# Weights from 64-bit floats: upper bits of the low word by ScalarE, and the first gates' low halves by TensorE

## The chip, the cores and the metric

One NeuronCore of a Trainium2 chip runs the whole program. The metric is device time in microseconds (us), from launch to end. The engines are named as the profile names them: PE (TensorE, matmuls; PEld are its weight loads), DVE (VectorE), ACT (ScalarE), POOL (GpSimd) and SP (SyncE, which issues the transfers).

## The reference, cut to what matters

```python
def _attn_ref(q, k, v, alpha):                 # B=4, H=8, S=768, D=48
    for t in range(S):
        state = alpha[:, :, t, :, None] * state + np.einsum('bhd,bhe->bhde', k[:, :, t], v[:, :, t])
        y[:, :, t] = np.einsum('bhd,bhde->bhe', q[:, :, t], state)

def _moe_ref(x, w_in, conv_w, w_out):          # d_model 384, d_ff 1024, 3 taps
    h = np.maximum(x @ w_in, 0.0)
    # conv_out: 3 taps of h along the sequence, one weight per feature and tap
    gate = 1.0 / (1.0 + np.exp(-conv_out))
    return h * gate @ w_out

def _moe2_ref(x, g_ln, w_ch1, w_ch2):          # hidden 1536
    xn = (x - mu) / np.sqrt(var + 1e-06) * g_ln
    return x + np.maximum(xn @ w_ch1, 0.0) @ w_ch2
```

The three functions follow one another. The four weight matrices and `conv_w` reach the kernel as 64-bit floats; the kernel makes 32-bit floats of them itself.

## The kernel before, in words

The 3072 rows of the sequence are 12 blocks of 256. Attention runs ahead of the blocks in 24 chunks of 128 rows: two scans and a reciprocal on DVE (L399, L405, L415), products on POOL (L411, L419), scores, outputs and state on PE (L441, L509, L525). Each block then goes through two halves. The first half has 8 pieces of 128 features (`moe1_a`, `moe1_gate`, `moe1_split`): nine products into a PSUM bank `h` (L595), relu in that bank (L608), one tap by ACT (L612) and two by DVE (L616), sigmoid (L635), `h` times gate in the bank (L639), a rounded upper half `gh` by ACT (L656), the rest `gl` by DVE (L661). Only then is the bank free, and there are three banks `h`. Six products per 128 features go into `acc` (L687). A norm and two transposes (L756) lead to the second half, with 12 pieces: nine products (L790), `gh` by ACT (L798), `gl` by DVE (L803), six products into `acc`.

All products use numbers split into a rounded upper half and a lower half. A weight matrix is cut in pieces of 768 columns: 4 of `w_in` (w1), 4 of `w_out` (w2), 6 each of `w_ch1` (w3) and `w_ch2` (w4), 20 in all. A piece is loaded as 64-bit numbers (L279) and converted (`from_f64`, `convert_weight`): ACT makes a scaled float of the high word (L254); DVE shifts it left by 3 (L257), joins the top 3 bits of the low word (L260) and the sign (L263); ACT rounds the upper half (L301). The lower half is a subtraction: for w1 and w2 by PE into PSUM with a copy by ACT (L305, L306, L309), for w3 and w4 by POOL (L312). Two buffers `z` hold pieces in work.

The order is written by a planner (`Plan`): every step has a price, a turn and its buffers, and steps are given to engines in the order of their turns as soon as their inputs and buffers are free by these prices. Each engine then runs its list strictly in that order. The turns come from the table of numbers at the top (`FIRST`, `LEAD`, `LOADS`, `CONVERT`, `WAIT` and so on).

Of the kernel before, what the change touches and what calls it, by code (L numbers as in the profile page):

```python
# [35 lines left out]
HB = 3  # L36
XB = 2
ZB = 2
GB = 3
RB, EB = 2, 2  # L40

SPLIT = 0
UNITS = (0, 0, 0), (0, 1, 0) 
XN = 1 
X1 = 2 
WAIT = 4
LAG = 5
FIRST = (-16,-15,-14,-4,2)
LEAD = 6
SPACING = 2  # L50
FETCH = 10
LOADS = -17, -12, -6, -5.5
LOAD_PACE = 1
CONVERT = (-13,-8,9,9)
CONVERT_PACE = 1, 1, 1
EARLY = 0
LATER = 0, 8
LOW2 = "pool"
LOWS = "pe", "pe", "pool", "pool"
# [144 lines left out]
def dve_us(n, rate=1):  # L204
    return 0.15 + 0.00104 * rate * n
# [11 lines left out]
def attn_moe_kernel(ctx: ExitStack, tc, qka, vv, qka_t, v_t, w_in, conv_w, w_out, g_ln, w_ch1, w_ch2, out):  # L217
# [32 lines left out]
    def from_f64(z, raw, n):  # L250

        low, high = raw[:, :n, 0], raw[:, :n, 1]
        zi = z.bitcast(I32)
        yield lambda: act.activation(out=z, in_=high.bitcast(F32), func=ACTF.Copy, scale=2.0 ** -112)  # L254

        def shift():
            dve.tensor_scalar(out=zi, in0=zi, scalar1=3, scalar2=None, op0=ALU.logical_shift_left)  # L257

        def more():
            dve.scalar_tensor_tensor(  # L260
                out=zi, in0=low, scalar=29, in1=zi, op0=ALU.logical_shift_right, op1=ALU.bitwise_or
            )
            dve.scalar_tensor_tensor(  # L263
                out=zi, in0=high, scalar=-(2 ** 31), in1=zi, op0=ALU.bitwise_and, op1=ALU.bitwise_or
            )

        yield shift
        yield more

    raw_w = {}  # L270

# [14 lines left out]
    def convert_weight(n, dst, j):  # L286
        m, w, z = PIECE * DM, (f"w{n}", j), ring("z", ZB)
        t = {}

        def first():  # L290
            t["z"] = wk.tile([128, m], F32, tag="z", name="z", bufs=ZB)
            raw = raw_w.pop((n, j)).rearrange("p j s f -> p (j s f)")
            t["f"] = list(from_f64(t["z"], raw.rearrange("p (n w) -> p n w", w=2), m))
            t["f"][0]()

        def high():
            t["w"] = weight_tile(n, j, F32R)
# [12 lines left out]

        def rest(engine):
            engine.tensor_tensor(out=t["w"][:, :, 1], in0=t["z"], in1=t["w"][:, :, 0], op=ALU.subtract)  # L312

        add("act", act_us(m), first, r=[w], new=[z])
        add("dve", dve_us(m, 0.5), lambda: t["f"][1](), w=[z], port=True)
        add("dve", 2 * dve_us(m), lambda: t["f"][2](), r=[w], w=[z], port=True)
        add("act", act_us(m), high, r=[z], w=[w])
        low = LOW2 if n > 2 and j >= F2 // 2 // PIECE else LOWS[n - 1]
        if low == "pe":
            for i in range(PIECE):  # L320
                b = ring("att", 2)
# [263 lines left out]
    def moe1_a(i, j):  # L585
        hb, cb = ring("h", HB), ring("cv", 2)
        t = h_t[i, j] = {"hb": hb, "cb": cb}

        def products():
            hi, lo = x_t[i]  # L590
            ps = bank("h", "h")
            n = 0
            for l, r in ((0, hi), (1, hi), (0, lo)):
                for k in range(K1):
                    pe.matmul(  # L595
                        out=ps[:, :T + 2], lhsT=w1[j][:, l, k * 128:(k + 1) * 128], rhs=r[:, k, :],
                        start=n == 0, stop=n == 3 * K1 - 1,
                    )
                    n += 1
            t["h"] = ps[:, :T + 2]  # L600

        def relu():
            if i < EARLY:
                ps = t["h"]
                t["h"] = wk.tile([128, T + 2], F32, tag="hs", name="hs", bufs=EB)
                act.activation(out=t["h"], in_=ps, func=ACTF.Relu)
            else:
                act.activation(out=t["h"], in_=t["h"], func=ACTF.Relu)  # L608
# [12 lines left out]
        xs = list(x_b[i]) if i in x_b else []
        add("pe", 9 * 0.000458 * (T + 2), products, r=xs + [("w1", j // PIECE)], new=[hb], mode="full")
        if i < EARLY:
            t["hb"] = ring("hs", EB)
            add("act", act_us(T), relu, r=[hb], new=[t["hb"]])
        else:
            add("act", act_us(T), relu, w=[hb])
        add("act", act_us(T, True), first_tap, r=[t["hb"]], new=[cb])
        add("dve", 2 * (dve_us(T) + 0.06), taps, r=[t["hb"]], w=[cb])

    def moe1_gate(i, j):
        t = h_t[i, j]

        def sigmoid():
            act.activation(out=t["cv"], in_=t["cv"], func=ACTF.Sigmoid)  # L635

        def times(engine):
            g = t["h"][:, 1:T + 1]
            engine.tensor_tensor(out=g, in0=g, in1=t["cv"], op=ALU.mult)  # L639

        add("act", act_us(T), sigmoid, w=[t["cb"]])
        if i < EARLY:
            add("pool", pool_us(T), lambda: times(pool), r=[t["cb"]], w=[t["hb"]], port=True)
        else:
            add("dve", dve_us(T), lambda: times(dve), r=[t["cb"]], w=[t["hb"]])
# [4 lines left out]
    def moe1_split(i, j):  # L650
        t = h_t.pop((i, j))
        m_b[0, i, j] = bh, bl = halves()

        def high():
            m_t[0, i, j] = [wk.tile([128, T], F32R, tag="gh", name="gh", bufs=GB), None]
            act.activation(out=m_t[0, i, j][0], in_=t["h"][:, 1:T + 1], func=ACTF.Copy)  # L656

        def rest(engine):
            hi = m_t[0, i, j][0]
            lo = m_t[0, i, j][1] = wk.tile([128, T], F32R, tag="gl", name="gl", bufs=GB)  # L660
            engine.tensor_tensor(out=lo, in0=t["h"][:, 1:T + 1], in1=hi, op=ALU.subtract)  # L661

        add("act", act_us(T), high, r=[t["hb"]], new=[bh])
        if i < EARLY:
            add("pool", pool_us(T), lambda: rest(pool), r=[t["hb"], bh], new=[bl], port=True)
        else:
            add("dve", dve_us(T), lambda: rest(dve), r=[t["hb"], bh], new=[bl])

    def parts_of(s, i):

# [76 lines left out]
    def ln3(i, t):  # L747
# [175 lines left out]
    def load_small():  # L923
# [234 lines left out]
```

## Time and profile before

| | us |
|---|---|
| median of 3 runs (689.48 to 691.96) | 691.35 |
| the profiled execution | 688.87 |
| its span, first to last instruction | 687.1 |
| PE busy | 643.6 (94%) |
| DVE busy | 449.5 (65%) |
| ACT busy | 308.8 (45%) |
| POOL busy | 127.1 (19%) |

Busy shares are means over the span. Whether an engine sets the pace is read per stretch: which engine is full there, and on whom PE waits. A matmul's duration includes its way through the pipeline, so what one costs in a stream is the distance between the starts of two.

### The profile page before, as it was taken

To read this page: it belongs to the slowest core of one execution; us is meant where nothing else is said; L and a number is where in the kernel's file an instruction comes from. 1 tells how busy PE (TensorE), PEld (TensorE's weight loads), DVE (VectorE), ACT (ScalarE), POOL (GpSimd) and SP (SyncE) were. 2 spreads that over 40 slices of the span, in tenths; PEclk is the share of its full clock that TensorE was granted. 3 is DMA by queue.
4 is the path that set the end of the run, shared out by engine and by line. 5 is a ranking of instruction groups with operands and counts; after the bars stand their busy time and mean duration, and the time that the engine had idled before them with its cause. 6 is when DMAs were issued, how large, how long until landed. Compare 5 with 4: busy or idle time off the path is not lost.

```text
span 687.1 us, 14178 instructions
## 1 busy us (share of the span) xinstructions
PE 643.6 (94%) x5754; PEld 609.2 (89%) x5754; DVE 449.5 (65%) x902; ACT 308.8 (45%) x752; POOL 127.1 (19%) x193
## 2 busy tenths in 40 slices
PE   3779868889999999999999999999999999999995
PEld 2557858789999999999999999999999999999994
DVE  5989998989749549639549548648648547365221
ACT  2758775445436336335335335345245245253210
POOL 4143244451320121201111111201201100000000
PEclk9999998979999999999999999999999999999998
DMA  9999101012310211110120111110100000000000
GB/s 303 307 359 298 55 0 42 16 41 79 98 56 24 58 57 39 57 42 24 56 56 25 57 57 44 57 37 30 55 14 24 18 1 24 1 24 1 2 24 27
DMA packets 15738, 44.51 MB, mean 65 GB/s; under 512 B 1473, under 2 KB 4673, under 8 KB 15665
## 3 DMA queue, kind: packets, MB, share of 16 engines
q1 hardware_dynamic: 15664, 43.52, 20.1%
q8 instruction: 47, 0.77, 0.5%
q14 instruction: 27, 0.21, 0.1%
HBM read 38.80 MB, written 4.72 MB: 63 GB/s over the span
## 4 chain that ended last, share of the span: by engine, by line
PE 83%; DVE 8%; ACT 3%; issue 2%; DMA 1%; POOL 1%; SPq 0%; ACTq 0%; DVEq 0%
PE acc L687 34%; PE h L790 22%; PE h L595 14%; PE y L509 5%; PE s L441 4%; DVE z L260 2%; DVE z L263 2%; PE u L525 2%; PE h L756 1%; DVE cv L616 1%; DMA raw<-in_qka 1%; PE kt L465 1%; DVE gl L661 1%; DVE z L257 1%; PE low L305 1%
## 5 line engine op out<-in xcount | busy, mean ns | idle before, releaser
L687 PE MATMUL acc<-w,gh 128*128 128x384 f32 x960 | 254.7, 346 | 3.0 <-ACT w L301 1.5
L687 PEld LDWEIGHTS acc<-w,gh 128*128 128x128 f32 x960 | 163.2, 190 | 7.3 <-ACT w L301 1.7
L687 PE MATMUL acc<-w,gl 128*128 128x384 f32 x480 | 162.5, 339 | 0.1
L803 DVE SCALAR_TENSOR_TENSOR gl<-h,gh 128x256 fp32r<-128x256 f32 x144 | 60.7, 423 | 153.7 <-ACT gh L798 153.0
L798 ACT ACTIVATE gh<-h 128x256 fp32r<-128x256 f32 x144 | 55.2, 384 | 195.9 <-PE acc L687 184.5
L790 PE MATMUL h<-xnh,w 128*128 128x256 f32 x864 | 129.2, 285 | 1.5 <-POOL w L312 1.5
L790 PEld LDWEIGHTS h<-xnh,w 128*128 128x128 f32 x864 | 119.4, 190 | 3.3 <-POOL w L312 1.8
L616 DVE SCALAR_TENSOR_TENSOR cv<-h,cw,cv 128x256 f32<-128x256 f32 x192 | 91.8, 481 | 28.8 <-ACT cv L612 24.4
L687 PEld LDWEIGHTS acc<-w,gl 128*128 128x128 f32 x480 | 91.1, 190 | 0.7 <-DVE gl L803 0.7
L595 PE MATMUL h<-xh,w 128*128 128x258 f32 x576 | 86.9, 286 | 4.7 <-DVE gl L661 2.9
L595 PEld LDWEIGHTS h<-xh,w 128*128 128x128 f32 x576 | 78.2, 189 | 8.8 <-DVE gl L661 4.8
L790 PE MATMUL h<-xnl,w 128*128 128x256 f32 x432 | 75.3, 283 | 0.0
L790 PEld LDWEIGHTS h<-xnl,w 128*128 128x128 f32 x432 | 62.2, 190 | 0.0
L635 ACT ACTIVATE cv<-cv 128x256 f32<-128x256 f32 x96 | 39.7, 415 | 37.1 <-DVE cv L616 36.8
L608 ACT ACTIVATE h<-h 128x258 f32<-128x258 f32 x96 | 35.5, 370 | 46.0 <-PE h L595 45.5
L402 POOL COPY ends<-later 112x4 f32<-112x4 f32 x24 | 4.9, 203 | 261.1 <-DVE later L399 259.5
L595 PE MATMUL h<-xl,w 128*128 128x258 f32 x288 | 50.1, 282 | 0.0
L612 ACT ACTIVATE cv<-h,cw 128x256 f32<-128x256 f32 x96 | 45.5, 474 | 1.9
L639 DVE TENSOR_TENSOR h<-h,cv 128x256 f32<-128x256 f32 x96 | 40.5, 424 | 5.9 <-ACT cv L635 4.0
L661 DVE TENSOR_TENSOR gl<-h,gh 128x256 fp32r<-128x256 f32 x96 | 40.1, 417 | 5.6 <-ACT gh L656 5.2
L656 ACT ACTIVATE gh<-h 128x256 fp32r<-128x256 f32 x96 | 36.7, 383 | 10.3 <-DVE h L639 9.1
L595 PEld LDWEIGHTS h<-xl,w 128*128 128x128 f32 x288 | 41.3, 190 | 0.0
(87 smaller groups left out, 742.6 us busy)
## 6 DMA issues: line engine op xcount, KB each, us to landing
raw<-in_qka SPq DMA_DIRECT2D x23, 673.8 KB, 4.8
w<-in_moe_w_ch SPq DMA_DIRECT2D x12, 768.0 KB, 16.5
vraw<-in_vv SPq DMA_DIRECT2D x24, 256.0 KB, 2.8
out<-x SPq DMA_DIRECT2D x11, 384.0 KB, 2.5
w<-in_moe_w_in SPq DMA_DIRECT2D x4, 768.0 KB, 11.4
w<-in_moe_w_out SPq DMA_DIRECT2D x4, 768.0 KB, 13.5
raw<-in_qka SPq DMA_DIRECT2D x1, 448.0 KB, 3.8
out<-x SPq DMA_DIRECT2D x2, 192.0 KB, 3.3
```

The source lines that it names most:

```text
L595: pe.matmul(out=ps[:, :T + 2], lhsT=w1[j][:, l, k * 128:(k + 1) * 128], rhs=r[:, k, :], start=n == 0, stop=n == 3 * K1 - 1,)
L608: act.activation(out=t["h"], in_=t["h"], func=ACTF.Relu)
L612: act.activation(out=t["cv"], in_=t["h"][:, 0:T], func=ACTF.Copy, scale=cw[:, 0, j:j + 1])
L616: dve.scalar_tensor_tensor(out=t["cv"], in0=t["h"][:, k:k + T], scalar=cw[:, k, j:j + 1], in1=t["cv"], op0=ALU.mult, op1=ALU.add,)
L635: act.activation(out=t["cv"], in_=t["cv"], func=ACTF.Sigmoid)
L639: engine.tensor_tensor(out=g, in0=g, in1=t["cv"], op=ALU.mult)
L656: act.activation(out=m_t[0, i, j][0], in_=t["h"][:, 1:T + 1], func=ACTF.Copy)
L661: engine.tensor_tensor(out=lo, in0=t["h"][:, 1:T + 1], in1=hi, op=ALU.subtract)
L687: pe.matmul(out=acc_t[s, i][t][:, :DM], lhsT=l[:, ts], rhs=w[j][:, r], start=j in firsts and n == 0, stop=j + 1 in lasts and n == 2,)
L790: pe.matmul(out=ps[:, :T], lhsT=w3[j][:, l, k * 128:(k + 1) * 128], rhs=r[:, k, :], start=n == 0, stop=n == 3 * K1 - 1,)
L798: act.activation(out=m_t[1, i, j][0], in_=u["ps"][:, :T], func=ACTF.Relu)
L803: dve.scalar_tensor_tensor(out=lo, in0=u["ps"][:, :T], scalar=0.0, in1=hi, op0=ALU.max, op1=ALU.subtract)
```

## The change

ACT takes over the top bits of the low word: it reads byte 3 of each 8-byte number, multiplies by 1/32 with an offset that makes the rounding a floor, and writes the integer over the low word. DVE's shift goes into the join, so two DVE instructions are left of three. In the first two blocks the lower half of `h` times gate is made by PE, which subtracts `gh` in the bank (`less`), and ACT copies the result to `gl`; the product with the gate is written from column 0 on. The lower halves of the first three pieces of w4 go from POOL to PE and ACT. There is a fourth buffer for `gh` and `gl`, and the table of turns has other numbers. The branch `EARLY`, off before, is gone.

```diff
-GB = 3
-RB, EB = 2, 2
+GB = 4
+RB = 2
-WAIT = 4
+WAIT = 6
-LEAD = 6
+LEAD = 4
...
-LOADS = -17, -12, -6, -5.5
+LOADS = -17, -16, -4, -9.5
-CONVERT = (-13,-8,9,9)
...
+CONVERT = -17, -9, 8, 10
+BY_PE = 2, 0
-LOWS = "pe", "pe", "pool", "pool"
+LOWS = "pe", "pe", "pool", "pe" 
...
-        def shift():
-            dve.tensor_scalar(out=zi, in0=zi, scalar1=3, scalar2=None, op0=ALU.logical_shift_left)
-
-        def more():
+        def top():
+            byte = raw[:, :n, :].bitcast(U8)[:, :, 3]
+            act.activation(out=low, in_=byte, func=ACTF.Copy, scale=1 / 32, bias=-15.5 / 32)
+
+        def join():
             dve.scalar_tensor_tensor(
-                out=zi, in0=low, scalar=29, in1=zi, op0=ALU.logical_shift_right, op1=ALU.bitwise_or
+                out=zi, in0=zi, scalar=3, in1=low, op0=ALU.logical_shift_left, op1=ALU.bitwise_or
             )
...
+    def less(ps, high):
+
+        pe.matmul(out=ps, lhsT=minus, rhs=high, start=False, stop=True, skip_group_check=True)
...
-            g = t["h"][:, 1:T + 1]
-            engine.tensor_tensor(out=g, in0=g, in1=t["cv"], op=ALU.mult)
+            dve.tensor_tensor(out=t["h"][:, :T], in0=t["h"][:, 1:T + 1], in1=t["cv"], op=ALU.mult)
...
+        if i < BY_PE[0] and not plan.direct:
+            add("pe", 0.000458 * T, take, r=[bh], w=[t["hb"]], mode="full")
+            add("act", act_us(T), lambda: rest(True), r=[t["hb"]], new=[bl])
         else:
```

ACT's list, where the third pieces of w1 and w2 are converted (`w1_2` and `w2_2` with a serial number; raw and converted tile have numbers of their own). Before:

```order
L254 ACTIVATE z_341<-w1_2_113 128x768
L309 ACTIVATE w2_1_331<-low_333 128x384
L309 ACTIVATE w2_1_331<-low_347 128x384
L254 ACTIVATE z_355<-w2_2_156 128x768
L388 ACTIVATE raw_183,low_68<-raw_183 112x4x128
L301 ACTIVATE w1_2_380<-z_341 128x2x384
```

The same pieces in the changed kernel (L257 is the scaled float, L261 the new instruction, L306 the upper half, L314 the copy of a lower half):

```order
L257 ACTIVATE z_326<-w1_2_122 128x768
L261 ACTIVATE w1_2_122<-w1_2_122 128x768
L306 ACTIVATE w2_1_333<-z_310 128x2x384
L314 ACTIVATE w2_1_333<-low_337 128x384
L306 ACTIVATE w1_2_350<-z_326 128x2x384
L314 ACTIVATE w2_1_333<-low_345 128x384
L257 ACTIVATE z_361<-w2_2_127 128x768
L314 ACTIVATE w1_2_350<-low_355 128x384
L261 ACTIVATE w2_2_127<-w2_2_127 128x768
```

Each piece now has one instruction more on ACT between the scaled float and the upper half, and DVE's join waits for it.

PE's list in the second block's first half, before: products into `h` (L595) alternate with products into `acc` (L687).

```order
L595 MATMUL h_923<-xh_443,w1_1_313 128x258 x6
L595 MATMUL h_923<-xl_452,w1_1_313 128x258 x3
L687 MATMUL acc_571<-w2_3_544,gh_906 128x384 x2
L687 MATMUL acc_571<-w2_3_544,gl_917 128x384
L687 MATMUL acc_572<-w2_3_544,gh_906 128x384 x2
L687 MATMUL acc_572<-w2_3_544,gl_917 128x384
L595 MATMUL h_956<-xh_443,w1_1_313 128x258 x6
L595 MATMUL h_956<-xl_452,w1_1_313 128x258 x3
```

The same place in the changed kernel (L354 is `less`, L604 the products into `h`, L310 and L311 the lower half of a piece of w4):

```order
L354 MATMUL h_883<-gh_963,minus_62 128x256
L604 MATMUL h_982<-xh_477,w1_1_302 128x258 x6
L604 MATMUL h_982<-xl_479,w1_1_302 128x258 x3
L310 MATMUL low_999<-z_930,ident_61 128x384
L311 MATMUL low_999<-w4_1_993,minus_62 128x384
L354 MATMUL h_906<-gh_997,minus_62 128x256
L604 MATMUL h_1016<-xh_477,w1_2_350 128x258 x6
L604 MATMUL h_1016<-xl_479,w1_2_350 128x258 x3
L354 MATMUL h_948<-gh_1026,minus_62 128x256
```

`h_982` takes the bank of `h_883`, and `h_1016` that of `h_906`: the nine products stand right behind the `less` on the bank that they reuse.

DVE's list at the last three pieces, before (L803 is `gl` of the second half):

```order
L257 TENSOR_SCALAR z_1423<-z_1423 128x768
L405 RECIPROCAL from_end_79<-later_1419 112x4
L260 SCALAR_TENSOR_TENSOR z_1423<-w4_4_520,z_1423 128x768
L263 SCALAR_TENSOR_TENSOR z_1423<-w4_4_520,z_1423 128x768
...
L257 TENSOR_SCALAR z_1484<-z_1484 128x768
L415 SCALAR_TENSOR_TENSOR a_1501<-raw_723,from_end_79 112x516
L260 SCALAR_TENSOR_TENSOR z_1484<-w4_5_566,z_1484 128x768
L263 SCALAR_TENSOR_TENSOR z_1484<-w4_5_566,z_1484 128x768
```

And in the changed kernel (L264 and L267 are the two joins, L736 belongs to the norm, L816 is `gl`):

```order
L264 SCALAR_TENSOR_TENSOR z_1390<-z_1390,w4_4_376 128x768
L267 SCALAR_TENSOR_TENSOR z_1390<-w4_4_376,z_1390 128x768
L736 SCALAR_TENSOR_TENSOR xn_1431<-x1_1305,mv_1374,gl_65 128x384
L816 SCALAR_TENSOR_TENSOR gl_1470<-h_1413,gh_1449 128x256
L264 SCALAR_TENSOR_TENSOR z_1411<-z_1411,w3_5_548 128x768
L267 SCALAR_TENSOR_TENSOR z_1411<-w3_5_548,z_1411 128x768
```

The shifts are gone, and the scans (L399, L415) that stood between the last pieces stand elsewhere.

## Rows read from the trace of the kernel before

**Rows 1.** Windows: busy time and count per engine, granted clock, DMA share, GB/s

```profile
core 0: us, PE busy (x) PEld busy (x) DVE busy (x) ACT busy (x) POOL busy (x), PEclk, DMA share, GB/s
0.00:46.20 46.20, 28.25 (x285) 19.52 (x285) 36.98 (x50) 22.28 (x39) 15.27 (x35) 0.93 0.99 327
46.20:97.70 51.50, 45.23 (x417) 39.58 (x418) 46.99 (x92) 38.58 (x88) 15.84 (x18) 1.00 0.48 148
97.70:149.10 51.40, 40.56 (x293) 37.47 (x291) 45.16 (x64) 24.08 (x47) 26.88 (x19) 0.83 0.07 20
149.10:687.10 538.00, 529.62 (x4764) 512.58 (x4762) 320.34 (x697) 223.84 (x580) 69.13 (x123) 1.00 0.13 39
```

**Rows 2.** PE's waits, first 150 us: line, releaser, total us, times, longest

```profile
PE h L756 <- DVE gl L661: 6.2, 1, 6.2
...
PE acc L687 <- ACT w L301: 1.5, 1, 1.5
...
PE h L790 <- POOL w L312: 1.5, 1, 1.5
...
PE acc L687 <- POOL w L312: 1.4, 1, 1.4
```

**Rows 3.** Windows of the two longest stretches at half the clock

```profile
102.80:109.60 6.80, 4.73 (x17) 4.64 (x18) 5.35 (x12) 3.48 (x9) 2.77 (x4) 0.50 0.01 4
136.90:147.20 10.30, 7.85 (x29) 7.56 (x30) 8.88 (x8) 2.92 (x4) 6.46 (x4) 0.50 0.00 0
```

**Rows 4.** Groups by line: count, busy us, mean ns, idle before and releaser

```profile
L661 DVE TENSOR_TENSOR gl<-h,gh 128x256 fp32r<-128x256 f32 x96 | 40.1, 417 | 5.6 <-ACT gh L656 5.2
...
L656 ACT ACTIVATE gh<-h 128x256 fp32r<-128x256 f32 x96 | 36.7, 383 | 10.3 <-DVE h L639 9.1 <-PE acc L687 1.1
...
L312 POOL TENSOR_TENSOR w<-z,w 128x768 fp32r<-128x768 f32 x12 | 25.5, 2126 | 39.8 <-ACT w L301 39.8
L263 DVE SCALAR_TENSOR_TENSOR z<-w,z 128x768 int32<-128x768 int32 x20 | 23.6, 1178 | 0.7
...
L260 DVE SCALAR_TENSOR_TENSOR z<-w,z 128x768 int32<-128x768 int32 x20 | 22.0, 1099 | 0.2
L254 ACT ACTIVATE z<-w 128x768 f32<-128x768 f32 x20 | 18.2, 910 | 9.2 <-DMA w<-in_moe_w_in 5.3 <-POOL w L312 3.9
...
L301 ACT ACTIVATE w<-z 128x768 fp32r<-128x768 f32 x20 | 16.8, 841 | 13.5 <-DVE z L263 13.4
...
L257 DVE TENSOR_SCALAR z<-z 128x768 int32<-128x768 int32 x20 | 12.7, 640 | 1.2 <-ACT z L254 1.2
...
L309 ACT ACTIVATE w<-low 128x384 fp32r<-128x384 f32 x16 | 7.8, 490 | 3.9 <-PE low L306 3.9
```

**Rows 5.** Timeline of ACT: the first piece of a weight (start, duration)

```profile
12.42 0.89 ACT L254 ACTIVATE z<-w 128x768 f32<-128x768 f32 x1 [5.25 <-DMA w<-in_moe_w_in]
```

**Rows 6.** Timeline of PE: neighbouring starts of like products

```profile
23.57 0.81 PE L305 MATMUL low<-z,ident 128*128 128x384 f32 x2
...
24.39 0.84 PE L305 MATMUL low<-z,ident 128*128 128x384 f32 x2
...
111.98 0.88 PE L790 MATMUL h<-xnh,w 128*128 128x256 f32 x6
...
113.05 0.87 PE L790 MATMUL h<-xnh,w 128*128 128x256 f32 x6
```

**Rows 7.** Timeline: one gate, last products to `gh` and `gl`

```profile
89.35 0.52 PE L595 MATMUL h<-xl,w 128*128 128x258 f32 x3
...
95.38 0.37 ACT L656 ACTIVATE gh<-h 128x256 fp32r<-128x256 f32 x1
...
95.82 0.42 DVE L661 TENSOR_TENSOR gl<-h,gh 128x256 fp32r<-128x256 f32 x1
```

More of the change, by code (lines that the diff above doesn't have):

```diff
@@ L11 @@
 I32 = mybir.dt.int32
+U8 = mybir.dt.uint8
 ACTF = mybir.ActivationFunctionType
@@ L45 @@
 X1 = 2
-WAIT = 4
+WAIT = 6
 LAG = 5
-FIRST = (-16,-15,-14,-4,2)
-LEAD = 6
+FIRST = -16, -15, -14, -4, 2
+LEAD = 4
 SPACING = 2
-FETCH = 10
-LOADS = -17, -12, -6, -5.5
+FETCH = 12
+LOADS = -17, -16, -4, -9.5
 LOAD_PACE = 1
-CONVERT = (-13,-8,9,9)
-CONVERT_PACE = 1, 1, 1
-EARLY = 0
+CONVERT = -17, -9, 8, 10
+CONVERT_PACE = 1.25, 1, 1
+BY_PE = 2, 0
 LATER = 0, 8
 LOW2 = "pool"
-LOWS = "pe", "pe", "pool", "pool"
+LOWS = "pe", "pe", "pool", "pe"
 class Plan:
@@ L253, in from_f64, with first @@
         zi = z.bitcast(I32)
-        yield lambda: act.activation(out=z, in_=high.bitcast(F32), func=ACTF.Copy, scale=2.0 ** -112)
-        def shift():
-            dve.tensor_scalar(out=zi, in0=zi, scalar1=3, scalar2=None, op0=ALU.logical_shift_left)
-        def more():
+        def first():
+            act.activation(out=z, in_=high.bitcast(F32), func=ACTF.Copy, scale=2.0 ** -112)
+        def top():
+            byte = raw[:, :n, :].bitcast(U8)[:, :, 3]
+            act.activation(out=low, in_=byte, func=ACTF.Copy, scale=1 / 32, bias=-15.5 / 32)
+        def join():
             dve.scalar_tensor_tensor(
-                out=zi, in0=low, scalar=29, in1=zi, op0=ALU.logical_shift_right, op1=ALU.bitwise_or
+                out=zi, in0=zi, scalar=3, in1=low, op0=ALU.logical_shift_left, op1=ALU.bitwise_or
             )
@@ L265, in more @@
             )
-        yield shift
-        yield more
+        yield first
+        yield top
+        yield join
     raw_w = {}
@@ L314, in convert_weight @@
         add("act", act_us(m), first, r=[w], new=[z])
-        add("dve", dve_us(m, 0.5), lambda: t["f"][1](), w=[z], port=True)
+        add("act", act_us(m), lambda: t["f"][1](), w=[w])
         add("dve", 2 * dve_us(m), lambda: t["f"][2](), r=[w], w=[z], port=True)
@@ L602, in relu @@
         def relu():
[L603 to L608, printed above, removed]
+            act.activation(out=t["h"], in_=t["h"], func=ACTF.Relu)
         def first_tap():
@@ L622, in moe1_a @@
         add("pe", 9 * 0.000458 * (T + 2), products, r=xs + [("w1", j // PIECE)], new=[hb], mode="full")
[L623 to L627, printed above, removed]
+        add("act", act_us(T), relu, w=[hb])
         add("act", act_us(T, True), first_tap, r=[t["hb"]], new=[cb])
@@ L635, in sigmoid, with times @@
             act.activation(out=t["cv"], in_=t["cv"], func=ACTF.Sigmoid)
-        def times(engine):
-            g = t["h"][:, 1:T + 1]
-            engine.tensor_tensor(out=g, in0=g, in1=t["cv"], op=ALU.mult)
+        def times():
+            dve.tensor_tensor(out=t["h"][:, :T], in0=t["h"][:, 1:T + 1], in1=t["cv"], op=ALU.mult)
         add("act", act_us(T), sigmoid, w=[t["cb"]])
[L642 to L645, printed above, removed]
+        add("dve", dve_us(T), times, r=[t["cb"]], w=[t["hb"]])
     def halves():
@@ L655, in high, with rest, take @@
             m_t[0, i, j] = [wk.tile([128, T], F32R, tag="gh", name="gh", bufs=GB), None]
-            act.activation(out=m_t[0, i, j][0], in_=t["h"][:, 1:T + 1], func=ACTF.Copy)
-        def rest(engine):
-            hi = m_t[0, i, j][0]
+            act.activation(out=m_t[0, i, j][0], in_=t["h"][:, :T], func=ACTF.Copy)
+        def rest(by_pe):
+            hi, g = m_t[0, i, j][0], t["h"][:, :T]
             lo = m_t[0, i, j][1] = wk.tile([128, T], F32R, tag="gl", name="gl", bufs=GB)
-            engine.tensor_tensor(out=lo, in0=t["h"][:, 1:T + 1], in1=hi, op=ALU.subtract)
+            if by_pe:
+                act.activation(out=lo, in_=g, func=ACTF.Copy)
+            else:
+                dve.tensor_tensor(out=lo, in0=g, in1=hi, op=ALU.subtract)
+        def take():
+            less(t["h"][:, :T], m_t[0, i, j][0])
         add("act", act_us(T), high, r=[t["hb"]], new=[bh])
-        if i < EARLY:
-            add("pool", pool_us(T), lambda: rest(pool), r=[t["hb"], bh], new=[bl], port=True)
+        if i < BY_PE[0] and not plan.direct:
+            add("pe", 0.000458 * T, take, r=[bh], w=[t["hb"]], mode="full")
+            add("act", act_us(T), lambda: rest(True), r=[t["hb"]], new=[bl])
         else:
-            add("dve", dve_us(T), lambda: rest(dve), r=[t["hb"], bh], new=[bl])
+            add("dve", dve_us(T), lambda: rest(False), r=[t["hb"], bh], new=[bl])
     def parts_of(s, i):
@@ L766, in high, with rest @@
             act.activation(out=xnT_t[i][0][:, :, ts], in_=source(), func=ACTF.Copy)
-        def rest():
+        def rest(by_pe):
             if t == 0:
@@ L771, in rest, with take @@
             hi, lo = (x[:, :, ts] for x in xnT_t[i])
-            dve.tensor_tensor(out=lo, in0=source(), in1=hi, op=ALU.subtract)
+            if by_pe:
+                act.activation(out=lo, in_=source(), func=ACTF.Copy)
+            else:
+                dve.tensor_tensor(out=lo, in0=source(), in1=hi, op=ALU.subtract)
+        def take():
+            less(source(), xnT_t[i][0][:, :, ts])
         add("pe", 0.35, turn, r=[xn_b[i]], new=[hb], mode="full")
@@ L776, in ln3 @@
         add("act", act_us(DM), high, r=[hb], **{key: [xnT_b[i][0]]})
-        add("dve", dve_us(DM), rest, r=[hb, xnT_b[i][0]], **{key: [xnT_b[i][1]]})
+        if i < BY_PE[1] and not plan.direct:
+            add("pe", 0.000458 * DM, take, r=[xnT_b[i][0]], w=[hb], mode="full")
+            add("act", act_us(DM), lambda: rest(True), r=[hb], **{key: [xnT_b[i][1]]})
+        else:
+            add("dve", dve_us(DM), lambda: rest(False), r=[hb, xnT_b[i][0]], **{key: [xnT_b[i][1]]})
     def moe2_a(i, j):
@@ L932, in load_small @@
         add("act", act_us(24), lambda: t["f"][0](), r=[("cwr", 0)], w=[("cw", 0)])
-        add("dve", 0.18, lambda: t["f"][1](), w=[("cw", 0)])
+        add("act", act_us(24), lambda: t["f"][1](), w=[("cwr", 0)])
         add("dve", 0.36, lambda: t["f"][2](), r=[("cwr", 0)], w=[("cw", 0)])
```

## The prediction

> **What bounds the kernel now.** I read the busy time by windows first and moved the borders until each stage had one limit [rows 1]. From 149.1 us on PE is busy 529.6 of 538 us, and the rest is the tail after its last product: there only PE work counts. Before that are three stages. A (0 to 46.2) ends with the first product into `h`: the DMA queues are 0.99 busy, ACT and DVE convert w1 and w2. B (46.2 to 97.7) holds the 16 pieces of the first halves of blocks 0 and 1: DVE is busy 47.0 of 51.5 us, 0.91, ACT 38.6, PE 45.2. C (97.7 to 149.1) has the norms and the second half of block 0 while the last pieces of w3 and w4 are converted: DVE 45.2 of 51.4, PE 40.6. Then the list of PE's waits [rows 2]: in C it waits 6.2 us for one `gl` that holds a bank, and 1.5, 1.4 and 1.5 us for converted weights, all behind DVE's queue. After these waits the granted clock was 0.50, so 1.2 of 2.4 GHz, in two stretches in which PE was busy 4.73 and 7.85 us [rows 3]; half of that, 6.3 us, is lost. So of C's 51.4 us, 40.6 - 6.3 = 34.3 are work at full clock and 17.1 are idle or lost to the clock. C is where something can be won.
>
> **The change part by part.** DVE loses 20 shifts of 640 ns, 12.8 us, and 16 `gl` of 417 ns, 6.7 us: 19.5 together [rows 4]. The two joins of a piece keep their 1.10 and 1.18 us: the first has the same two inputs with places changed. It is not the dearest third of the old three that goes, but the cheapest instruction.
>
> ACT gains 20 `top` instructions. Their form, bytes at a step of 8 read and words at a step of 8 written, is not in the trace. The nearest rows are L254, which reads words at that step, 910 ns, and L301, which reads packed, 841 ns [rows 4]. I take 910. Below, nothing in these rows lets 768 elements cost less than 841; above, I allow twice, 1.8 us, since no row here writes at that step. [...] The 16 copies to `gl` are priced as L656, 383 ns, and six copies of lower halves as L309, 490 ns. Together ACT gets 18.2 + 6.1 + 2.9 = 27.2 us, almost all of it before 149 us.
>
> PE gains 16 `less`. Nine products of that width start 1.07 us after the nine before them, so 0.12 us each, 1.9 us; the six lower halves of w4 start 0.82 us apart, 4.9 us [rows 6]. That is 6.8 us more work that all counts in the end. POOL loses three subtractions of 2.13 us [rows 4], and DVE with them some fights for the shared port (the joins' means of 1.10 and 1.18 are held up by it).
>
> Now by stage, with the changed order.
>
> A. From the first landed piece at 12.4 us [rows 5] ACT has 20.0 of 33.8 us of work before: stage A's 22.3 [rows 1] less 2.3 ahead of that moment. The new list puts in the same stretch eight `top` (7.3), two more scaled floats (1.8), two more upper halves (1.7), three more copies of lower halves (1.5) and a guard (0.8): 33.1 us, a full queue. The chain of a piece is also longer, since the join waits for `top` behind the scaled float, with two buffers `z`. At 0.93 full ACT gets through it 35.6 us after 12.4, at 48. DVE and DMA give no earlier end. I take +2 us, between -1 (ACT no bound: DMA remains) and +5 (0.87 full).
>
> B. ACT's 38.6 us get seven `top` (6.4), 14 copies to `gl` (5.4), one lower half (0.5), two sigmoids and a `gh` that come in before the border (1.2), less one scaled float and one guard (-1.7): 50.4 us. Rows that follow each other at once overlap by about 0.1 us (busy time counts that once), so about 48. DVE falls to about 37 (seven shifts, 4.5, and 14 `gl`, 5.8, off 47.0), so ACT is now the full queue here. If it runs as full as DVE does now, 0.91, B takes 52.7 us; I take +1.5, between -3.5 (ACT without a gap) and +13 (the first rival).
>
> C. ACT and DVE both have room: five pieces are converted in this stage, each without its shift (-3.2 us), and the scans no longer stand between them. PE's work grows by three `less` and two lower halves (0.4 + 1.6) and some 0.9 of a chunk that changes its place: 37.2 us. What is idle or lost falls from 17.1; the wait for the `gl` and those for weights lose most of their cause, and with shorter waits the half-speed stretches go too. I leave 5 us of the 17, between 1 and 13: C takes 42.2 us, -9.2, between -13 and -1.
>
> After C. Of PE's 6.8 us of additions and the shifted chunk some 7.8 lie ahead of this border, so 1 us less is left behind it; there PE is full as now. DVE runs at 320 of 538 us there, which no `gl` of blocks 2 to 11 changes.
>
> The sum is 2 + 1.5 - 9.2 - 1 = -6.7 us. It is made against the profiled span of 687.1 (688.87 with what lies around it); that execution lies 2.5 us under the median, so I set the same difference against 691.35: 684.6, say 684.
>
> **The rivals.** 1. Slower: the bank is handed over through two more queues. Before, a bank was free 0.5 us after `gh` by DVE alone; in one gate the end of `gh` came 5.9 us behind the last products, and the end of `gl` 6.4 us [rows 7]. Now `gh` must reach PE's queue, and ACT must copy; the nine products on the same bank stand right behind their `less`, so PE waits for the copy with nothing to do. If a `top` is in front of the copy, that is 0.91 + 0.38 = 1.3 us, at 13 banks that are reused 17 us. B's 45.2 + 2.4 us of PE work would take 64.6 us, +13; with A +4, C -6.2 and the rest -1 the time is 701. It decides from a B of 63 us on. For it speaks that ACT is nearly full in B; against it, that in the changed order most products into `h` have six or more groups of about 1.1 us (the nine products of [rows 6]) between them and their `less`, as long as the chain of that gate. A `top` at 1.8 us ends at the same place, with ACT 14 us longer in A and B. The rule of the Trainium skill (ScalarE: Activation LUTs, Rules for kernel authors), that additions and multiplications belong on VectorE and not on ScalarE, speaks on this side: by it the moved work is dear where it goes. The trace agrees on the price of one piece, 910 ns for 640.
>
> 2. No change: ACT is the new bound in A and B at 0.87 full (+4 and +3.5), and C loses 8 us to waits (-6.2): 691.35 + 0.3, so 692. For it: what DVE sheds (19.5 us) is less than what ACT takes (27.2).
>
> 3. Much faster: ACT's overlaps let A stay and B shrink by 3.5, and C has almost no wait (-13): with the 1 us, -17.5, so 674. For it: all idle time of PE in C goes back to DVE's queue, which is emptied most there.
>
> **How the numbers follow.** A difference of 0.5%, 3.5 us, is about what a measurement of this kernel can tell from none. The forecast, -4 to -13 us, has 0.46, much faster 0.20, no change 0.20, slower 0.14. So faster is 0.66, the same 0.20, slower 0.14. The range goes from 673, where the third rival lies, to 696, half way into the first; the forecast's own is 678 to 687.
>
> **What would show each step.** In the windows of the changed kernel: the first product into `h` at 47 to 49 us; ACT busy above 0.88 until the 16th product into `h`, at 98 to 102; DVE below 0.85 there. `top` near 0.91 us. The last piece joined before 130 us, the third block's first product at 139 to 145 us, PE without idle time behind it, and no half-speed stretch longer than 7 us in C. It would be wrong if PE's waits in B go to ACT's copy of `gl` for over 12 us, if `top` takes over 1.2 us, or if PE still waits for `w` of the last pieces.

## The result and the profile after

The changed kernel takes 684.25 us (median of four runs, 680.59 to 685.02); the kernel before took 691.44 beside it. The ratio is 0.9896, with a 95% interval of 0.9861 to 0.9931. In another group of runs it was 685.79 us, ratio 0.9915 (0.9885 to 0.9945), so the change is worth 6 to 7 us. The forecast was 684; it is the sum of terms that miss by up to 6 us and offset each other. The profiled execution took 685.02 us, with a span of 683.2.

Windows of the changed kernel, with borders at the same events as in [rows 1]: the first product into `h`, the end of the 16th piece, the third block's first product.

```profile
0.00:53.90 53.90, 35.99 (x295) 23.16 (x295) 37.35 (x46) 32.58 (x56) 18.85 (x37) 0.91 1.00 338
53.90:108.80 54.90, 48.60 (x432) 43.20 (x433) 46.25 (x80) 46.70 (x107) 18.95 (x22) 0.97 0.26 82
108.80:146.50 37.70, 36.95 (x349) 34.36 (x348) 33.82 (x51) 27.64 (x56) 17.38 (x13) 1.00 0.15 45
146.50:683.20 536.70, 528.21 (x4719) 511.90 (x4717) 315.11 (x691) 221.65 (x578) 68.76 (x120) 0.99 0.12 37
```

Against [rows 1], A is 7.7 us longer, B 3.4 longer, C 13.7 shorter and the rest 1.3 shorter: -3.9 between these two executions. That of before lay 2.5 us under its median and that of after 0.8 above, which makes the 7.2 of the medians. C is now nearly all PE work, at full clock: 36.95 of 37.7 us. PE's waits in B and C together:

```profile
PE h L604 <- ACT gl L658: 3.3, 5, 1.2
PE h L354 <- ACT gh L652: 2.5, 1, 2.5
PE h L604 <- POOL xh L580: 1.1, 1, 1.1
PE y L518 <- issue: 0.7, 1, 0.7
...
```

The last of these rows is all that is left in C. The four waits of [rows 2], 10.6 us, are gone. The groups of the new and moved operations, over the first 160 us:

```profile
L267 DVE SCALAR_TENSOR_TENSOR z<-w,z 128x768 int32<-128x768 int32 x20 | 25.1, 1256 | 0.7
...
L264 DVE SCALAR_TENSOR_TENSOR z<-z,w 128x768 int32<-128x768 int32 x20 | 20.9, 1047 | 7.5 <-ACT w L261 7.5
...
L261 ACT ACTIVATE w<-w 128x768 int32<-128x768 uint8 x20 | 18.3, 917 | 0.0
...
L314 ACT ACTIVATE w<-low 128x384 fp32r<-128x384 f32 x22 | 10.7, 488 | 6.2 <-PE low L311 6.0
...
L658 ACT ACTIVATE gl<-h 128x256 fp32r<-128x256 f32 x16 | 6.1, 381 | 1.0 <-PE h L354 0.3
```

`top` takes 917 ns, as L254 did (910, [rows 4]). The Trainium skill (ScalarE: Activation LUTs, What ACT_TABLE_LOAD costs) gives 186 ns plus 0.833 ns per element with constant scale and bias, for fp32 and bf16 alike; for 768 elements that is an estimate of 826 ns. This row, which reads bytes, does not agree, and the measurement decides. The two joins together take 2.30 us, before 2.28. The new cost that no price list held is in the second row: VectorE sits idle for 7.5 us until a `top` has come (1.2 us before, on the scaled float, [rows 4]).

### The profile page after: what moved, and what is told of

It reads as the page before. It is cut to its first block, busy times and chain, and to the rows that moved or that the text cites. A ratio compares the mean times of both kernels' runs of the same rounds, so it can differ in the third digit from the quotient of the medians.

```text
span 683.2 us, 14211 instructions
## 1 busy us (share of the span) xinstructions
PE 649.7 (95%) x5788; PEld 612.6 (90%) x5788; DVE 432.5 (63%) x865; ACT 328.6 (48%) x795; POOL 123.9 (18%) x190
## 4 chain that ended last, share of the span: by engine, by line
PE 89%; DVE 4%; ACT 3%; DMA 1%; issue 1%; POOL 0%; SPq 0%; ACTq 0%
PE acc L690 37%; PE h L803 23%; PE h L604 15%; PE y L518 5%; PE s L450 4%; PE u L534 2%; PE low L310 1%; PE h L759 1%; DMA raw<-in_qka 1%; PE kt L474 1%; DVE z L267 1%; DVE z L264 1%; ACT w L261 1%; ACT z L257 0%; ACT w L314 0%
## 5 line engine op out<-in xcount | busy, mean ns | idle before, releaser
L690 PE MATMUL acc<-w,gh 128*128 128x384 f32 x960 | 250.9, 342 | 0.0
L690 PEld LDWEIGHTS acc<-w,gh 128*128 128x128 f32 x960 | 160.9, 188 | 3.4 <-issue 0.8
L816 DVE SCALAR_TENSOR_TENSOR gl<-h,gh 128x256 fp32r<-128x256 f32 x144 | 60.4, 422 | 153.8 <-ACT gh L811 151.9
L803 PE MATMUL h<-xnh,w 128*128 128x256 f32 x864 | 127.5, 283 | 0.0
L803 PEld LDWEIGHTS h<-xnh,w 128*128 128x128 f32 x864 | 118.4, 188 | 1.0 <-DVE a L424 0.4
L604 PE MATMUL h<-xh,w 128*128 128x258 f32 x576 | 87.4, 288 | 4.4 <-ACT gl L658 3.3
L604 PEld LDWEIGHTS h<-xh,w 128*128 128x128 f32 x576 | 79.5, 191 | 7.7 <-ACT gl L658 4.5
L803 PE MATMUL h<-xnl,w 128*128 128x256 f32 x432 | 74.9, 282 | 0.0
L612 ACT ACTIVATE h<-h 128x258 f32<-128x258 f32 x96 | 35.7, 372 | 61.7 <-PE h L604 59.2
L803 PEld LDWEIGHTS h<-xnl,w 128*128 128x128 f32 x432 | 61.6, 188 | 0.0
L604 PE MATMUL h<-xl,w 128*128 128x258 f32 x288 | 50.4, 283 | 0.0
L428 POOL TENSOR_TENSOR a<-raw,a 112x512 f32<-112x512 f32 x24 | 30.1, 1254 | 69.7 <-DVE a L424 68.4
L604 PEld LDWEIGHTS h<-xl,w 128*128 128x128 f32 x288 | 41.6, 191 | 0.2 <-POOL xl L580 0.2
```

Of the source, the lines that this page charges most:

```text
L604: pe.matmul(out=ps[:, :T + 2], lhsT=w1[j][:, l, k * 128:(k + 1) * 128], rhs=r[:, k, :], start=n == 0, stop=n == 3 * K1 - 1,)
L690: pe.matmul(out=acc_t[s, i][t][:, :DM], lhsT=l[:, ts], rhs=w[j][:, r], start=j in firsts and n == 0, stop=j + 1 in lasts and n == 2,)
L803: pe.matmul(out=ps[:, :T], lhsT=w3[j][:, l, k * 128:(k + 1) * 128], rhs=r[:, k, :], start=n == 0, stop=n == 3 * K1 - 1,)
L816: dve.scalar_tensor_tensor(out=lo, in0=u["ps"][:, :T], scalar=0.0, in1=hi, op0=ALU.max, op1=ALU.subtract)
```

## The experiments

Times are medians; ratios are to the kernel before, run beside each group. Stages are read from one profiled execution of each kernel, which can lie 2 us off its median (that of experiment 10 lies 2.2 above, those of experiments 5 and 9 lie 2.1 and 1.8 below). So a difference of 2 us in one stage shows nothing by itself.

**1 and 2. Operations and table apart.** The table (LOADS, CONVERT, CONVERT_PACE, WAIT, LEAD, FETCH) was put back in the changed kernel, and put into the kernel before, there with the fourth buffer for `gh` and `gl` (GB = 4).

```diff
 e1: the changed kernel            e2: the kernel before
-WAIT = 6                          -WAIT = 4
+WAIT = 4                          +WAIT = 6
-CONVERT = -17, -9, 8, 10          -CONVERT = (-13,-8,9,9)
+CONVERT = -13, -8, 9, 9           +CONVERT = -17, -9, 8, 10
...
```

> The changed kernel's operations (upper bits by ScalarE, gl by TensorE and ScalarE, w4's lower halves by TensorE) in the order that the old table (LOADS, CONVERT, WAIT, LEAD, FETCH) gives. Theory O (the operations make the gain: VectorE's queue is emptied by 19.5 us before 149 us): most of it is here already, 683 to 687 us, and the first product into h stays near 48 us. Rival T (the table makes it, by bringing conversions forward into stage A, and the operations only shift work): no gain, 690 to 695 us, first product near 48 us, stage C over 48 us as before.

> The kernel before with the new table alone (LOADS, CONVERT, CONVERT_PACE, WAIT, LEAD, FETCH, GB = 4). Theory O: VectorE was 0.91 full in B and has now more of it in A: 690 to 697 us, the first product into h later than 50 us. Rival T: 683 to 687 us. If the lateness of stage A (53.9 us in the changed kernel) belongs to the table and not to ScalarE's new step, the first product is at 52 us or later here as well; if it belongs to the step, it is at 46 to 50 us.

New operations with the old table: 689.92 us, ratio 0.9987 (0.9977 to 0.9997). New table with the old operations: 688.19, 0.9956 (0.9944 to 0.9969). Neither theory holds: each half alone gives 0.1 and 0.4%, both together 0.9 to 1.0%. Stages A, B and C, of e1 and then of e2:

```profile
0.00:48.80 48.80, 28.54 (x289) 18.52 (x289) 33.40 (x41) 27.96 (x50) 17.26 (x36) 0.97 0.99 330
48.80:113.40 64.60, 55.61 (x441) 48.64 (x442) 50.64 (x87) 52.07 (x116) 20.06 (x23) 0.89 0.37 114
113.40:149.00 35.60, 34.54 (x297) 32.48 (x297) 31.75 (x46) 25.20 (x54) 16.00 (x13) 1.00 0.09 28
```

```profile
0.00:50.30 50.30, 31.07 (x292) 19.70 (x293) 38.94 (x52) 23.45 (x42) 16.52 (x37) 0.93 0.99 336
50.30:105.40 55.10, 45.93 (x408) 41.09 (x407) 49.53 (x94) 39.05 (x89) 15.83 (x17) 0.93 0.34 106
105.40:148.20 42.80, 37.46 (x280) 35.31 (x278) 41.70 (x58) 20.31 (x40) 24.01 (x17) 0.89 0.08 23
```

Stage A, 46.2 before, is 48.8 with the operations alone and 50.3 with the table alone: each makes it later, and which does more is not shown by 1.5 us between two profiles. With the operations alone C has hardly a gap (34.54 of 35.6), but B has grown by 13.1 us. Some 6 of these are the granted clock, 0.89 in that B and 1.00 before: 12.1 of PE's 55.6 us ran at half clock (59.2 to 66.0 and 76.4 to 83.2 us). With the table alone VectorE is 0.97 full in C (41.70 of 42.8).

**3. `less` undone.**

```diff
-BY_PE = 2, 0
+BY_PE = 0, 0
```

> The changed kernel with gl of blocks 0 and 1 by VectorE again (BY_PE = 0, 0), all else as changed. Theory O: VectorE takes back 16 times 417 ns = 6.7 us, PE loses 16 less of 0.12 us = 1.9 us and its waits for gl and gh in stage B (3.3 + 2.5 us): the two cancel, 682 to 686 us. Rival L (handing gl to PE is what emptied VectorE's queue in C, where one wait for gl had cost 6.2 us): 687 to 691 us, with a wait of PE for gl of over 3 us in C.

691.47 us, ratio 1.0006 (0.9993 to 1.0019): all of the gain is gone. The rival's time came (0.5 us above its range), but not by its mechanism. Stages B, C and the rest:

```profile
54.00:112.70 58.70, 48.78 (x421) 42.50 (x422) 52.04 (x98) 47.26 (x104) 18.98 (x23) 0.96 0.36 105
112.70:149.40 36.70, 32.99 (x276) 31.52 (x276) 28.77 (x44) 22.27 (x44) 15.96 (x15) 0.97 0.03 8
149.40:689.30 539.90, 531.57 (x4785) 514.59 (x4783) 318.54 (x695) 222.14 (x578) 69.65 (x117) 1.00 0.12 37
```

C is not longer, and PE waits there 2.1 us for a `gl`, under the 3 named. B is longer (58.7 for 54.9), with VectorE busy 52.0 us of it and 46.3 in the changed kernel; C then holds 4 us less PE work, which is left for later (the rest takes 3.2 us longer).

**4. `top` undone, the shift on VectorE again.**

```diff
+        if n in BY_DVE:   # 1, 2, 3, 4
+            add("dve", dve_us(m, 0.5), lambda: t["f"][1](), w=[z], port=True)
+        else:
             add("act", act_us(m), lambda: t["f"][1](), w=[w])
```

> The changed kernel with the shift by VectorE again for all weights, three operations to a piece (top is left only for the small convolution weights). Theory O: VectorE gets 20 times 640 ns = 12.8 us back, ScalarE loses 18.3 us; stage A ends 3 to 5 us earlier, and B and C together take 8 to 10 us more: 687 to 691 us. Rival K (the longer chain first, top, join in A costs as much as the shift did): 680 to 685 us.

689.34 us, ratio 0.9974 (0.9961 to 0.9987), in the range of theory O. The first product came at 50.6 us, 3.3 earlier; B took 56.4 and C 43.2 with VectorE 0.96 full in it, together 7.0 us more than in the changed kernel, for the 8 to 10 of the theory.

**5. Three buffers `z`.**

```diff
-ZB = 2
+ZB = 3
```

> The changed kernel with three buffers z in place of two. Theory Z (stage A is long because a piece now holds its z through first, top, join, upper half and lower half, and the third piece must wait for a z): the first product into h comes at 49 to 51 us instead of 53.9, and the time is 680 to 683 us. Rival Q (in A it is the order within VectorE's queue: joins stand between the steps of chunk 2's scan, which the first product needs): the first product stays at 53 us or later, 683 to 687 us.

The first product came at 48.7 us, as theory Z said, but the time was 687.13, ratio 0.9952 (0.9934 to 0.9969): no gain. The timeline of ScalarE shows the buffer: the second and third piece's scaled floats in the changed kernel, then with three buffers:

```profile
14.94 0.93 ACT L257 ACTIVATE z<-w 128x768 f32<-128x768 f32 x1
24.89 0.96 ACT L257 ACTIVATE z<-w 128x768 f32<-128x768 f32 x1
```

```profile
15.30 0.93 ACT L257 ACTIVATE z<-w 128x768 f32<-128x768 f32 x1
18.53 0.90 ACT L257 ACTIVATE z<-w 128x768 f32<-128x768 f32 x1
```

Stage B of that kernel is 59.4 us for 54.9, and the border behind it, 108.1, is where it was:

```profile
48.70:108.10 59.40, 50.30 (x438) 44.12 (x437) 47.39 (x82) 49.49 (x115) 21.38 (x21) 0.97 0.40 121
```

**6. `top` for w3 and w4 alone.** The branch of experiment 4 with BY_DVE = 1, 2.

> The changed kernel with top for w3 and w4 alone; the eight pieces of w1 and w2 have their shift on VectorE again. Theory S (top costs 3 us in A, where each piece's chain is waited for, and gains in B and C, where VectorE is full): first product at 50 to 51 us, B and C as in the changed kernel, 680 to 683 us. Rival (VectorE is what is full in A too, since the scans of chunk 2 stand behind the joins; the shifts push work into B): no gain, 685 to 689 us.

685.27 us, ratio 0.9933 (0.9914 to 0.9952), which the measurement does not tell from the changed kernel. The first product came at 51.0, 2.9 us earlier; B took 58.3, 3.4 more; C 37.4. So it was neither: A is shorter by about the price that theory S gave `top` there, and B gave it back.

**7. w4's lower halves by GpSimd again.**

```diff
-LOWS = "pe", "pe", "pool", "pe" 
+LOWS = "pe", "pe", "pool", "pool" 
```

> The changed kernel with the first six lower halves of w4 by GpSimd again (LOWS as before): PE loses about 4.9 us of products, ScalarE six pairs of copies of 490 ns. Theory W (GpSimd's 2.1 us subtraction and its share of the port hold up w4's pieces, and PE waits for them in C): 686 to 690 us, with PE waits for w of GpSimd of 2 us or more. Rival F (C has no wait for weights left to remove, so PE work alone counts): 680 to 682 us.

687.88 us, ratio 0.9957 (0.9942 to 0.9971): 2 to 4 us slower, though PE has some 4.9 us less to do (the prediction's price of these products). Stage C, and then PE's waits in it:

```profile
108.30:145.70 37.40, 32.62 (x276) 30.62 (x275) 33.95 (x50) 25.12 (x50) 20.30 (x17) 1.00 0.10 27
```

```profile
PE h L759 <- DVE xnl L778: 2.3, 1, 2.3
PE h L759 <- ACT gl L658: 1.5, 1, 1.5
```

C is as long as in the changed kernel with 4.3 us less PE work in it. The waits are for a norm's `xnl` and a `gl`, not for weights of GpSimd as theory W had it; why these came late here is open, since the planner moves other steps too. What is shown is that taking these products away shortens neither C nor the whole, so in the changed kernel they stand in time that PE does not fill without them.

**8. w1's pieces at their old turns.**

```diff
-CONVERT = -17, -9, 8, 10
-CONVERT_PACE = 1.25, 1, 1 
+CONVERT = -13, -9, 8, 10
+CONVERT_PACE = 1, 1, 1
```

> The changed kernel with w1's pieces at their old turns and pace (CONVERT -13 in place of -17, pace 1 in place of 1.25), the rest of the new table kept. Theory Q (the pieces brought forward stand in front of chunk 2's scan): first product at 50 to 52 us, 681 to 684 us. Rival (pulling conversions into A is what leaves C empty of waits): first product earlier, but C 3 to 5 us longer, 686 to 689 us.

691.04 us, ratio 0.9995 (0.9974 to 1.0017). The first product came at 51.3, 2.6 us earlier, and B ended at 109.7, 0.9 later; C:

```profile
109.70:153.40 43.70, 39.93 (x346) 37.19 (x344) 35.43 (x51) 29.11 (x59) 19.13 (x15) 0.96 0.14 39
```

The rival was right in kind, an earlier A and a longer C, but its prices were too small: C is longer by 6.0 us for its 3 to 5, and 691.04 is above its 686 to 689. Of the 6.0 us, PE is busy in 3.0 (in part at a lower clock, 0.96 for 1.00) and idle in the other 3.0. That the pieces in front of chunk 2's scan cost time in A, as theory Q says, fits the first product (1.5 us ahead of that in experiment 9, too, so hardly more than the spread of one profile), and it is worth nothing in the time.

**9, 10 and 11. Loads with the order held.** Every undoing above lets the planner reorder all engines. In experiments 10 and 11 nothing moves: beside each copy to `gl` stands one instruction on VectorE, or on ScalarE, whose result nobody reads. The ninth is the changed kernel itself.

```diff
                 act.activation(out=lo, in_=g, func=ACTF.Copy)
+                if not plan.direct:
+                    dve.tensor_tensor(out=junk, in0=from_one[:, :2, :128], in1=from_one[:, 2:, :128], op=ALU.subtract)   # e10
+                    act.activation(out=junk, in_=from_one[:, :2, :128], func=ACTF.Copy)                                  # e11
```

> The changed kernel as it is, beside the three others of this group. Every theory expects 683 to 686 us; it is the measure for the two loads below and says whether three buffers z (687.1 us) and top for w3 and w4 alone (685.3 us) differ from it.

> The changed kernel in its own order, and beside each of the 16 copies to gl one subtraction by VectorE of the same width between constants, into a tile that nobody reads: VectorE's 6.7 us of gl are back, TensorE and ScalarE keep theirs, and no instruction changes its place. Theory V (VectorE's load in stage B is the limit, and the gain of the part with less is that it was taken off): 688 to 692 us. Rival M (the limit is when each step comes in the queues; VectorE has idle time for 6.7 us more): 684 to 686 us, and the 7 us that came back when less was undone belong to the new order.

> The same for ScalarE: one more copy of 256 columns behind each copy to gl, 16 times some 380 ns = 6.1 us, no instruction moved. Theory A (ScalarE is what bounds stage B of the changed kernel): B longer by 5 us or more, 688 to 691 us. Rival (ScalarE has gaps in B, 0.85 full): 684 to 686 us.

The changed kernel took 685.79 us (684.04 to 686.33), with VectorE's load 688.88 (687.73 to 691.03), with ScalarE's 686.92 (680.94 to 688.09). By the ratios (0.9915 here, 0.9952 and 0.9933 there) three buffers `z` are no gain over the changed kernel, and `top` for w3 and w4 alone is not told from it. Stage B in the three, and PE's longest waits in it, in this order:

```profile
52.80:107.70 54.90, 48.59 (x431) 43.26 (x432) 46.13 (x80) 46.64 (x107) 18.95 (x22) 0.97 0.29 89
...
PE h L604 <- ACT gl L658: 3.3, 5, 1.1
PE h L354 <- ACT gh L652: 2.5, 1, 2.5
```

```profile
54.70:113.80 59.10, 49.77 (x432) 43.09 (x433) 51.75 (x92) 47.46 (x106) 20.16 (x22) 0.97 0.27 80
...
PE h L605 <- ACT gl L659: 4.8, 6, 1.3
PE h L355 <- ACT gh L653: 4.0, 2, 2.5
```

```profile
53.80:111.10 57.30, 50.76 (x432) 44.62 (x433) 46.75 (x80) 50.07 (x119) 19.04 (x22) 0.94 0.25 78
...
PE h L605 <- ACT gl L659: 3.4, 5, 1.1
PE h L355 <- ACT gh L653: 2.5, 1, 2.5
```

VectorE's load costs: its fastest run is slower than the slowest run without it, by the medians 3.1 us for 16 subtractions of some 418 ns, 6.7 us. That is theory V, at about half the price of the load. PE's waits for `gl` and `gh` in B grew by 3.0 us, as did its idle time there (6.3 to 9.3 us). B is 4.2 us longer, but this sets the slowest of twelve executions against the fastest of six, so the medians are the better measure.

ScalarE's load, 16 copies of 412 ns, is not shown to cost anything: the medians differ by 1.1 us and the single runs overlap. B is 2.4 us longer in the profile, but not by waits. Those for `gl` and `gh` are as they were, and so is PE's idle time in B, 6.5 for 6.3 us. PE was busy 2.2 us longer, most of it because the granted clock was half (1.2 GHz) from 62.2 to 69.0 us, in experiment 9 only from 62.2 to 65.6, with PE busy throughout in both; why is open. So theory A's 5 us are not there, and the rival's time (684 to 686 us) was missed by 0.9.

Of the 6 to 7 us that undoing `less` lost, then, some 3 can be VectorE's load; the rest goes with the order or the handing over, which no run here separates.

**12. Three buffers `z`, and `top` for w3 and w4 alone.** The edits of 5 and 6 together.

> Three buffers z, and top for w3 and w4 alone, the rest as changed. Each of the two alone brought the first product 3 to 5 us forward and gave it back in B. Theory G (what is won in A is always given back, since conversions, norms and the 16 pieces fill ScalarE and VectorE up to about 146 us): 684 to 688 us, third block's first product at 145 to 148 us. Rival (both together free ScalarE in A by 7.3 us, and B gets shorter): 679 to 683 us.

682.75 us (five runs, 682.21 to 682.92), ratio 0.9872 (0.9840 to 0.9905); the changed kernel beside it had 684.04 to 686.33 in six runs. Here the two edits together gain 3 us. Against the changed kernel's first group (0.9896, with single runs of 680.59 and 683.49) it would be less than 2, and the intervals overlap, so the size of this gain is not settled. Its stages:

```profile
0.00:49.20 49.20, 33.37 (x298) 22.08 (x299) 41.24 (x54) 26.08 (x47) 16.99 (x37) 0.93 0.99 336
49.20:105.80 56.60, 48.54 (x430) 43.26 (x429) 48.34 (x81) 45.69 (x109) 18.75 (x22) 0.94 0.38 122
105.80:142.70 36.90, 35.65 (x303) 33.38 (x302) 33.37 (x48) 26.64 (x54) 15.28 (x12) 1.00 0.09 27
```

Of the 3.6 us that A gained against experiment 9, B gave back 1.7 and not all. The forecast time of the rival came, its mechanism half: ScalarE has 5.7 us less in A, but B is not shorter. Each edit alone gained nothing, the two together this much; why was not measured.

## Why the prediction was right, and which of its terms were not

**Prices.** 910 ns for `top` (917), 383 for the copies to `gl` (381), 490 for those of lower halves (488), and joins that keep their cost (2.30 for 2.28 us) were right. The upper bound of 1.8 us was far off.

**Stage A: +2, bound +5; measured +7.7, and +6.6 in experiment 9.** (At 0.87 full the prediction's own work gives +4, as its second rival has it, and not the +5 of its bound.) The step that failed is the full queue on ScalarE. The work was forecast nearly (33.1 us from 12.4 on), but ScalarE was busy 30.3 of the 41.6 us behind 12.3 (32.58 of the window, less about 2.3 ahead of it), 0.73 and not 0.93. A is set by a chain through two `z`, which the prediction names but gives no time, and by what stands in VectorE's queue between the steps of chunk 2, which the first product needs. The timeline of VectorE in the changed kernel, from chunk 2's scan to its `xl`, and then the same two ends before:

```profile
33.93 1.23 DVE L408 TENSOR_TENSOR_SCAN later<-raw,from_one 112x516 f32<-112x516 f32 x1
35.07 0.93 DVE L264 SCALAR_TENSOR_TENSOR z<-z,w 128x768 int32<-128x768 int32 x1
36.04 1.96 DVE L267 SCALAR_TENSOR_TENSOR z<-w,z 128x768 int32<-128x768 int32 x1
37.92 0.17 DVE L414 RECIPROCAL from_end<-later 112x4 f32<-112x4 f32 x1
...
38.86 1.28 DVE L424 TENSOR_TENSOR_SCAN a<-raw,from_end 112x516 f32<-112x516 f32 x1
...
41.44 1.62 DVE L264 SCALAR_TENSOR_TENSOR z<-z,w 128x768 int32<-128x768 int32 x1 [0.17 <-ACT w L261]
43.09 1.98 DVE L267 SCALAR_TENSOR_TENSOR z<-w,z 128x768 int32<-128x768 int32 x1
45.10 0.69 DVE L459 TENSOR_TENSOR pm<-s,mask 128x512 f32<-128x512 f32 x1
...
51.85 0.56 DVE L571 TENSOR_TENSOR xl<-y,xh 128x384 fp32r<-128x384 f32 x1
```

```profile
30.01 1.22 DVE L399 TENSOR_TENSOR_SCAN later<-raw,from_one 112x516 f32<-112x516 f32 x1
...
43.48 0.56 DVE L562 TENSOR_TENSOR xl<-y,xh 128x384 fp32r<-128x384 f32 x1
```

From scan to `xl` it takes 17.9 us, 13.5 before: the joins of three pieces and both scans of the next chunk stand in between, where it was two pieces and one scan. The scan itself starts 3.9 us later. The table alone makes A 4.1 us later (experiment 2), the operations alone 2.6 (experiment 1), and a third `z` takes back 4 to 5 (experiment 5). The prediction read the new list for ScalarE's work only, and not for what the list puts in front of chunk 2 on VectorE.

The miss was also cheap. In four kernels with an earlier first product (experiments 4, 5, 6 and 8) the time was not better, and only in experiment 12 it was. So A's length is no safe term of the sum by itself: what A leaves undone B must do.

**Stage B: +1.5; measured +3.4.** ScalarE's 48 us of work were right (46.7), its 0.91 was not: 0.85, near the 0.87 and +3.5 of the second rival. Nor was ScalarE the one full queue. VectorE was forecast at about 37 us in B and was busy 46.3, 0.84: the shifts and `gl` went as counted, but scans came in, and the prediction, which takes them out of C, counts them nowhere. VectorE's scans in B, before (46.2 to 97.7 us) and then changed (53.9 to 108.8):

```profile
L415 DVE TENSOR_TENSOR_SCAN a<-raw,from_end 112x516 f32<-112x516 f32 x1 | 2.0, 1982 | 0.0
...
L399 DVE TENSOR_TENSOR_SCAN later<-raw,from_one 112x516 f32<-112x516 f32 x1 | 1.2, 1220 | 0.0
```

```profile
L424 DVE TENSOR_TENSOR_SCAN a<-raw,from_end 112x516 f32<-112x516 f32 x3 | 4.6, 1526 | 0.0
L408 DVE TENSOR_TENSOR_SCAN later<-raw,from_one 112x516 f32<-112x516 f32 x3 | 4.0, 1335 | 0.0
```

That is 8.6 us for 3.2, or 5.4 of the 9 us that were missed; the rest is spread over small rows. Of the two more pairs one came out of C, the other belongs to a chunk that was brought forward. Experiment 10 shows that VectorE's work costs there; of ScalarE's, which the prediction took for the bound, experiment 11 does not show it. The first rival's waits are there, 3.3 us for `gl` in five and 2.5 for `gh` in one, far below its 17; its B of 63 us was not reached.

**Stage C: -9.2, bound -13; measured -13.7.** The waits for weights and for the `gl` went, and with them the half-speed stretches, as forecast; there was no time under full clock in C. PE's work was right, 36.95 us for 37.2. The term that missed is the idle time that was left in C: 5 us in the sum, 0.75 measured, below its bound of 1. That PE's added work "all counts in the end" does not hold as said either: in experiment 7 some 4.9 us of w4's products were taken away and the time did not fall but rose. The sum itself charged C with only 1.6 us of them. The last piece was not joined before 130 us but at 137.3; C needs no such early end, because PE has other work until then.

**The rest: -1; measured -1.3.** Right.

So the misses are +5.7 in A, +1.9 in B, -4.5 in C and -0.3 behind it: +2.8 between the two profiled executions, which the medians, 3.3 us further apart, took back. Three of its signs failed with them: the first product at 53.9 us for 47 to 49, ScalarE at 0.85 in B for above 0.88, and the third block's first product at 146.5 for 139 to 145. That the change is faster, and by which waits, was reasoned rightly: C was where something could be won, and its waits are gone. That VectorE's queue was their cause is borne out in part: undoing either of the parts that empty that queue (experiments 3 and 4) lost 4 us or more, but moved the order too, and experiment 3 lost it in B. Experiment 10, with the order held, puts some 3 us on VectorE's load. That the sum met the time to a microsecond was luck.

One thing the prediction did not have at all: it gave the operations and the table one common account. Alone they are worth 0.9 and 3 us, together 6 to 7; and undoing `less`, `top` or w4's products alone takes back 6 to 7, 4 to 5 and 2 to 4 of it, more in sum than there is. That each part keeps another queue from becoming the full one would explain this, but is not shown. A rival stays untested: every undoing keeps the changed kernel's table, and no run gives it a table of its own, so a part of each loss may be the table's misfit.

## What to carry to other kernels

When work moves between engines that are each some 0.85 full, price the stage by what a small load on each engine adds with the order held, not by how full a queue is: here 6.7 us more on VectorE cost 3 us, and 6.6 us more on ScalarE, as full by its busy time, cost nothing that was clear of noise. When an order moves work out of one stage, add it where it goes. Read a changed order for what now stands between the steps of the first thing that the bottleneck waits for, on every engine. A stage that begins later is no loss by itself, and work given to the bottleneck engine can be free where it stands in a wait. What decides is when the last stage that is not full ends, together with the work left for the full engine behind it: in experiment 7 C ended 0.8 us earlier, and the rest took 4.1 us longer.

## What the runs showed of the hardware beside that

- A ScalarE instruction that reads one byte of every eight and writes one word of every eight takes 917 ns for 768 elements, about as long as one that reads words at that step and writes packed (929 here, over the first 160 us).
- In the changed kernel the second join (L267) took 0.96 us at 46.70 us, where GpSimd had nothing to run, and 1.96 and 1.98 us at 36.04 and 43.09 us. GpSimd's `later` products (L420) ran at 36.01 (1.17 us) and 43.07 (1.19 us).
- With the same instructions in the same order up to the first product, four executions (the changed kernel, experiments 9, 10 and 11) began it at 53.9, 52.8, 54.7 and 53.8 us. Single runs of the changed kernel went from 680.59 to 686.33 us.
- A copy of 256 columns by ScalarE took 412 ns from one constant tile to another (112 partitions), and 381 from a bank to `gl` (128 partitions).
